# Loading 512 rows of w_down onto half of the partitions, in eight small transfers between the K and V loads

## The chip, the cores and the metric

One core of a Trainium2 chip runs the whole program. The metric is the device time of one execution in microseconds (us). On one core a run is called slow when it is over 1.5% above the fastest of its kernel, and such runs are left out of the ratios. The profile is one execution; its span is about 2 us shorter than the device time. All times on the traces' axis count from the start of the span. The traces name the engines PE (matmuls on TensorE), PEld (their weight loads), DVE (VectorE), ACT (ScalarE) and SP (which issues the loads). A "pair" is one weight load with the matmul that uses it.

## The reference

One decode step: 8 rows of x, attention with 32 query heads over the last 1024 positions of a K and V cache with 8 heads, and a gated feed-forward block whose result gates the attention.

```python
xn = layernorm(x)                                # [8, 1, 512]
q = xn @ wq                                      # 32 heads of 128
p = softmax(q @ k[last 1024].T / sqrt(128))      # 4 query heads share a K/V head
s = (p @ v) @ wo                                 # [8, 1, 512]
g = silu((gelu(xn @ w_gate) * (xn @ w_up)) @ w_down)   # F = 1792
out = x + s * g
```

Everything is bf16. There is little arithmetic and 47.5 MB to read: 16.8 MB each of K and V, 4.2 MB each of wq and wo, 1.8 MB each of w_gate, w_up and w_down.

## The kernel before

All loads are issued by one queue, in a fixed order: wq, then K and V in 1 MB pieces, then w_gate, w_up, the last V piece, w_down, and wo in four pieces. Eight semaphores take turns, so a load is issued when the one eight before it has landed.

```python
def load_rows(src, rows, r0, n, name):           # 128 partitions, n rows on each
    t = ring.tile([P, n, src.shape[1]], BF16, name=name, tag="slot")
    nc.sync.dma_start(out=t, in_=src.rearrange("(p r) n -> p r n", r=rows)[:, r0 : r0 + n, :])
    return t
...
wd_t = load_rows(B_w_down, FJ, 0, FJ, "wd_t")    # FJ = 14 rows on each partition
wo_t = [[load_rows(A_wo[: HT * Dh, :], WI, 0, WI, "wo_t")]]
wo_t.append([load_rows(A_wo[HT * Dh :, :], WI, 0, 8, "wo_t")])
...                                              # xr, then rows 8:13 and 13:16 of wo
```

Gate and up run as 14 groups of 128 columns of F. Since partition p of w_down's tile holds the rows 14p to 14p + 13, group j takes every 14th column:

```python
for w, wt in enumerate((wg_t, wu_t)):
    for j in range(FJ):
        for k in range(KD):                      # KD = 4
            nc.tensor.matmul(gu_ps[:, w, j, :],
                wt[:, k, :].rearrange("p (m j) -> p j m", j=FJ)[:, j, :],
                xnT[:, k, :], start=(k == 0), stop=(k == KD - 1))
```

GELU (ACT and DVE) makes hT of it, f_ps multiplies hT by w_down, and s_ps multiplies the attention output by wo, in the order in which wo's pieces land. Then two DVE instructions and the store end the program.

The softmax here doesn't subtract the row's maximum and nothing guards it: scores larger than these inputs give would overflow.

## Time and profile before

| | before |
|---|---|
| device time, median (range) | 122.9 us (122.73 to 123.09) |
| span of the profiled run | 121.0 us |
| DMA in the chain that ended last | 95% |
| PE busy | 85.1 us (70%) |
| last landing of the last wo piece | 116.86 us |
| gate starts / gate and up end | 96.26 / 104.06 us |
| s_ps ends | 117.44 us |

How to read it: 16 DMA engines work side by side (the page's DMA share is a mean over them). The records show sixteen increments of the semaphore for each load over 128 partitions, for the last wo piece from 113.73 to 116.86 us. They are read here as one from each engine, when its share of the load has landed: from 115 to 116 us, when nine of the sixteen have come (the ninth at 115.23), the DMA share is 0.42 of 16 engines, 6.7, and seven are missing. So the increments of one load say how far each engine is behind the others. These increments are in the trace's semaphore records; the page shows their sum only, as the way in which the DMA row falls at the end. The lines are in the prediction. No record numbers the engines. Where the texts give numbers, engines 0 to n - 1 are those that carry a load with n increments; that a load with more increments keeps the engines of one with fewer is the author's assumption.

### The profile page before, as it was taken

To read this page: it belongs to the slowest core of one execution; us is meant where nothing else is said; L and a number is where in the kernel's file an instruction comes from. 1 tells how busy PE (TensorE), PEld (TensorE's weight loads), DVE (VectorE), ACT (ScalarE), POOL (GpSimd) and SP (SyncE) were. 2 spreads that over 40 slices of the span, in tenths; PEclk is the share of its full clock that TensorE was granted. 3 is DMA by queue.
4 is the path that set the end of the run, shared out by engine and by line. 5 is a ranking of instruction groups with operands and counts; after the bars stand their busy time and mean duration, and the time that the engine had idled before them with its cause. 6 is when DMAs were issued, how large, how long until landed. Compare 5 with 4: busy or idle time off the path is not lost.

```text
span 121.0 us, 4362 instructions
## 1 busy us (share of the span) xinstructions
PE 85.1 (70%) x2015; PEld 78.7 (65%) x2030; DVE 69.8 (58%) x145; ACT 13.3 (11%) x22; POOL 1.4 (1%) x6
## 2 busy tenths in 40 slices
PE   0000699897879978879669693997969697845760
PEld 0000699896878977769669683896968597744640
DVE  3710036886947969669687592787859400398010
ACT  4500000110101101101101010110101100100000
POOL 4000000000000000000000000000000000000000
PEclk9999999999976999999999999599999955555555
DMA  4999999999999999999999999999999999999720
GB/s 100 423 433 433 401 420 420 433 423 431 417 428 423 420 431 415 428 423 428 423 420 417 431 425 428 428 423 420 417 449 433 418 419 440 438 417 409 316 88 3
DMA packets 6009, 47.75 MB, mean 395 GB/s; under 512 B 736, under 2 KB 744, under 8 KB 1000
## 3 DMA queue, kind: packets, MB, share of 16 engines
q1 hardware_dynamic: 5976, 47.47, 93.6%
q8 instruction: 16, 0.26, 0.8%
q10 hardware_dynamic: 16, 0.01, 0.0%
q14 instruction: 1, 0.01, 0.0%
HBM read 47.46 MB, written 0.01 MB: 392 GB/s over the span
## 4 chain that ended last, share of the span: by engine, by line
DMA 95%; DVE 0%; PE 0%; SPq 0%; issue 0%
DMA k_t<-in_A_k_cache_dram 51%; DMA wg_t<-in_B_w_gate_dram 18%; DMA wo_t<-in_A_wo_dram 17%; DMA wq_t<-in_A_wq_dram 10%; PE s_ps L355 0%; SPq L89 0%; DVE tmp L363 0%; DVE out_sb L365 0%; SPq L97 0%
## 5 line engine op out<-in xcount | busy, mean ns | idle before, releaser
L200 DVE COPY kT<-kT_ps 128x1024 bf16<-128x1024 bf16 x64 | 43.0, 692 | 16.0 <-PE kT_ps L196 16.0
L196 PE MATMUL kT_ps<-ident,k_t 128*128 128x128 bf16 x512 | 41.9, 230 | 11.8 <-DMA k_t<-in_A_k_cache_dram 11.8
L196 PEld LDWEIGHTS <-k_t 128*128 128x128 bf16 x512 | 31.8, 103 | 12.9 <-DMA k_t<-in_A_k_cache_dram 12.9
L213 PE MATMUL sc_ps<-qT,kT 128*128 128x16 bf16 x512 | 22.4, 170 | 0.5 <-DVE kT L200 0.4
L213 PEld LDWEIGHTS <-kT 128*128 128x128 bf16 x512 | 20.6, 98 | 2.9 <-issue 0.8
L220 ACT ACTIVATE pT<-sc_ps 128x512 bf16<-128x512 f32 x16 | 9.6, 597 | 80.8 <-PE sc_ps L213 80.8
L231 PEld LDWEIGHTS <-v_t 128*128 128x128 bf16 x512 | 15.5, 97 | 2.4 <-issue 0.8
L231 PE MATMUL oT_ps<-pT,v_t 128*128 128x16 bf16 x512 | 15.5, 170 | 1.3 <-issue 0.5
L235 DVE TENSOR_REDUCE sums<-sum_ps 128x16 f32<-128x512 f32 x16 | 11.0, 690 | 1.4 <-PE kT_ps L196 0.7
L178 PE MATMUL qT_ps<-xnT,wq_t 128*128 128x8 bf16 x128 | 3.7, 168 | 8.4 <-DMA wq_t<-in_A_wq_dram 8.4
L178 PEld LDWEIGHTS <-wq_t 128*128 128x128 bf16 x128 | 3.6, 104 | 8.5 <-DMA wq_t<-in_A_wq_dram 8.5
L207 PE MATMUL sc_ps<-mask,ident 128*128 128x512 bf16 x15 | 6.5, 430 | 0.0
L185 DVE CAST qT<-qT_ps 128x256 bf16<-128x256 f32 x1 | 0.4, 425 | 10.2 <-PE qT_ps L178 10.2
L355 PE MATMUL s_ps<-wo_t,oR 128*32 128x128 bf16 x128 | 4.2, 309 | 2.3 <-DMA wo_t<-in_A_wo_dram 2.3
L355 PEld LDWEIGHTS <-oR 128*32 128x32 bf16 x128 | 3.4, 139 | 2.9 <-issue 2.9
L290 DVE TENSOR_SCALAR z<-z 128x112 f32<-128x112 f32 x1 | 0.2, 219 | 8.4 <-ACT z L289 8.4
L239 DVE TENSOR_TENSOR oT<-oT_ps,sums 128x16 bf16<-128x16 f32 x16 | 3.7, 229 | 2.1 <-PE kT_ps L196 0.5
L238 DVE RECIPROCAL sums<-sums 128x16 f32<-128x16 f32 x16 | 4.0, 253 | 0.5
L279 PE MATMUL gu_ps<-xnT,wg_t 128*128 128x8 bf16 x56 | 3.5, 201 | 0.8 <-DMA wg_t<-in_B_w_gate_dram 0.8
L279 PE MATMUL gu_ps<-xnT,wu_t 128*128 128x8 bf16 x56 | 3.5, 202 | 0.7 <-DMA wu_t<-in_B_w_up_dram 0.7
L279 PEld LDWEIGHTS <-wg_t 128*128 128x128 bf16 x56 | 3.4, 161 | 0.9 <-DMA wg_t<-in_B_w_gate_dram 0.9
L279 PEld LDWEIGHTS <-wu_t 128*128 128x128 bf16 x56 | 3.5, 161 | 0.8 <-DMA wu_t<-in_B_w_up_dram 0.8
(51 smaller groups left out, 26.5 us busy)
## 6 DMA issues: line engine op xcount, KB each, us to landing
k_t<-in_A_k_cache_dram SPq DMA_DIRECT2D x16, 1024.0 KB, 20.5
v_t<-in_A_v_cache_dram SPq DMA_DIRECT2D x16, 1024.0 KB, 19.8
wq_t<-in_A_wq_dram SPq DMA_DIRECT2D x2, 2048.0 KB, 9.6
wo_t<-in_A_wo_dram SPq DMA_DIRECT2D x1, 2048.0 KB, 27.6
wg_t<-in_B_w_gate_dram SPq DMA_DIRECT2D x1, 1792.0 KB, 21.6
wu_t<-in_B_w_up_dram SPq DMA_DIRECT2D x1, 1792.0 KB
wd_t<-in_B_w_down_dram SPq DMA_DIRECT2D x1, 1792.0 KB, 25.2
wo_t<-in_A_wo_dram SPq DMA_DIRECT2D x1, 1024.0 KB, 27.4
```

Of the source, the lines that this page charges most:

```text
L178: nc.tensor.matmul(qT_ps[:, h, :], wq_t[k // 2][:, k % 2, h * Dh : (h + 1) * Dh], xnT[:, k, :], start=(k == 0), stop=(k == KD - 1),)
L196: nc.tensor.transpose(kT_ps[:, i * P : (i + 1) * P], k_t[b][:, h, t * TG + i, :], ident)
L200: nc.vector.tensor_copy(out=kT, in_=kT_ps)
L207: nc.tensor.matmul(sc[u].rearrange("p c h -> p (c h)"), ident, mask.rearrange("p c n j -> p (c n j)"), start=True, stop=False, skip_group_ ...
L213: nc.tensor.matmul(sc[u][:, t * TG + i, :], kTs[u, t][:, i * P : (i + 1) * P], qT[:, b, h * HS : (h + 1) * HS], start=False, stop=(t == NT ...
L220: nc.scalar.activation(out=pT[u], in_=sc[u], func=ACT.Exp, scale=inv_sqrt_dh)
L231: nc.tensor.matmul(oT_ps, v_t[b][:, h, c, :], pT[u][:, c, :], start=(c == 0), stop=(c == NCH - 1))
L235: nc.vector.tensor_reduce(out=sums, in_=sum_ps.rearrange("p c h -> p h c"), axis=AX.X, op=ALU.add)
L238: nc.vector.reciprocal(out=sums, in_=sums)
L239: nc.vector.tensor_tensor(out=oT[:, h, :, b], in0=oT_ps, in1=sums, op=ALU.mult)
L279: nc.tensor.matmul(gu_ps[:, w, j, :], wt[:, k, :].rearrange("p (m j) -> p j m", j=FJ)[:, j, :], xnT[:, k, :], start=(k == 0), stop=(k == K ...
L355: nc.tensor.matmul(s_ps[32 * q : 32 * (q + 1), :], oR[:, t, i, :], w[:, r, q * NW : (q + 1) * NW], start=(t == 0 and i == 0), stop=(t == N ...
```

## The change

The intent is to even out the ends of the DMA engines. Before, about half of them were done 3 us before the others (seven increments by 114.13 us, seven from 116.54 us on). 512 of w_down's rows now go by transfers of 8 partitions, which are carried by 8 engines only, and the 128-partition load of w_down shrinks by as much. The transfers are placed in the second half of the K and V loads, so that no engine runs far ahead. The partitions of each lie 4 apart.

```diff
-    FJ = F // P
+    FH = 64
+    FB = 8
+    FA = (F - FH * FB) // P
+    FJ = FA + FB
+    F0 = P * FA
...
+    wx_t = extra.tile([FH, FB, D], BF16, name="wx_t")
+    wx_rows = B_w_down[F0:, :].rearrange("(p j) n -> p (j n)", j=FB)
+    def load_extra(n):
+        p0 = 32 * (n // 4) + n % 4
+        nc.sync.dma_start(
+            out=wx_t[p0 : p0 + 29 : 4, :, :].rearrange("p j n -> p (j n)"),
+            in_=wx_rows[p0 : p0 + 29 : 4, :],
+        )
...
             load_cache(A_k_cache, u, k_t, "k_t")
+            if u >= NU - 8:
+                load_extra(u - (NU - 8))
             load_cache(A_v_cache, u - 1, v_t, "v_t")
...
-    wd_t = load_rows(B_w_down, FJ, 0, FJ, "wd_t")
+    wd_t = load_rows(B_w_down[:F0, :], FA, 0, FA, "wd_t")
...
+    nc.vector.memset(gu_ps[FH:P, :, FA:, :], 0.0)
...
+                if j < FA:
+                    cols = wt[:, k, :F0].rearrange("p (m j) -> p j m", j=FA)[:, j, :]
+                else:
+                    cols = wt[:, k, F0:].rearrange("p (m j) -> p j m", j=FB)[:, j - FA, :]
                 nc.tensor.matmul(
-                    gu_ps[:, w, j, :],
-                    wt[:, k, :].rearrange("p (m j) -> p j m", j=FJ)[:, j, :],
+                    gu_ps[: P if j < FA else FH, w, j, :],
+                    cols,
...
-                f_ps[...], hT[:, j, :], wd_t[:, j, q * NW : (q + 1) * NW],
+                f_ps[...],
+                hT[:, j, :] if j < FA else hT[:FH, j, :],
+                wd_t[:, j, ...] if j < FA else wx_t[:, j - FA, ...],
```

(One more line makes pT_pool 3 buffers instead of 4, for the room of wx_t.) Since the 512 rows lie on 64 partitions, 8 on each, the matmuls that make hT for them need weight loads of 64 columns, every eighth column of F.

More of the change, by code (lines that the diff above doesn't have):

```diff
@@ L63 @@
     ring = ctx.enter_context(tc.tile_pool(name="ring", bufs=10))
+    extra = ctx.enter_context(tc.tile_pool(name="extra", bufs=1))
     consts = ctx.enter_context(tc.tile_pool(name="consts", bufs=1))
     kT_pool = ctx.enter_context(tc.tile_pool(name="kT_pool", bufs=6))
-    pT_pool = ctx.enter_context(tc.tile_pool(name="pT_pool", bufs=4))
+    pT_pool = ctx.enter_context(tc.tile_pool(name="pT_pool", bufs=3))
     small = ctx.enter_context(tc.tile_pool(name="small", bufs=2))
@@ L326 @@
             nc.tensor.matmul(
-                f_ps[32 * q : 32 * (q + 1), :], hT[:, j, :], wd_t[:, j, q * NW : (q + 1) * NW],
+                f_ps[32 * q : 32 * (q + 1), :],
+                hT[:, j, :] if j < FA else hT[:FH, j, :],
+                wd_t[:, j, q * NW : (q + 1) * NW] if j < FA
+                else wx_t[:, j - FA, q * NW : (q + 1) * NW],
                 start=(j == 0), stop=(j == FJ - 1), tile_position=(0, 32 * q),
```

## The prediction

> **What bounds the kernel now.** I read the page's busy shares and slices first, then the chain of waits, the queues, the stretches of the last microseconds, the groups by shape, and the records of DMA packets and semaphore increments in the trace itself.
>
> The slices, the queues and the chain:
>
> ```profile
> PEclk9999999999976999999999999599999955555555
> DMA  4999999999999999999999999999999999999720
> ...
> q1 hardware_dynamic: 5976, 47.47, 93.6%
> q8 instruction: 16, 0.26, 0.8%
> q10 hardware_dynamic: 16, 0.01, 0.0%
> ...
> DMA 95%; DVE 0%; PE 0%; SPq 0%; issue 0%
> ```
>
> The 16 DMA engines are full from 3 us to about 113 us, and the chain is DMA for 95% of the span. PE is busy 70% and waits for data. So the kernel moves 47.5 MB at about 425 GB/s, and only bytes, or their division over engines, can move the end. The interesting part is the end of the DMA row: 9, 7, 2, 0. It doesn't drop at once. In stretches of 1 us (PE, PEld, DVE, ACT, POOL, clock, DMA share, GB/s):
>
> ```profile
> 113.00:114.00 1.00, 0.92 (x36) 0.73 (x28) 0.00 (x0) 0.00 (x0) 0.00 (x0) 0.50 0.77 302
> 114.00:115.00 1.00, 0.48 (x20) 0.48 (x23) 0.00 (x0) 0.00 (x0) 0.00 (x0) 0.50 0.54 223
> 115.00:116.00 1.00, 0.59 (x27) 0.40 (x20) 0.00 (x0) 0.00 (x0) 0.00 (x0) 0.50 0.42 170
> 116.00:117.00 1.00, 0.79 (x28) 0.59 (x31) 0.00 (x0) 0.00 (x0) 0.00 (x0) 0.50 0.15 58
> ```
>
> Half the engines are done by about 114 us, the other half at about 116.8 us (0.54 and 0.42 of 16 are 9 and 7 engines), although each was given the same bytes. The semaphore increments say it engine by engine. The last load (w_o, 384 KB) posts sixteen: seven at 113.73 to 114.13, one at 114.79, one at 115.23, seven at 116.54 to 116.86 us. For the K load at 15 us the sixteen lie within 0.4 us. The late ones split off one at a time in the first half, by 1.3 us each, and again in the second half, up to 3.1 us.
>
> The cause is in q8: 16 packets of 16 KB, about 6 us apart (18.6, 25.3, 31.3 ... 112.5, 117.0 us). Between two of them PE runs about 128 pairs of weight load and matmul, 256 instructions: they are PE's instruction fetches. Each takes about 0.93 us and slows the data packet beside it, and the engine that serves it falls 1.3 us behind. Fifteen fall before the data ends: seven engines get two, one gets one. That is exactly the late eight (seven at +2.8 us and the one at 115.23). The eighth early engine lost 0.7 us to one 8 KB fetch on another queue at 46.5 us.
>
> PE starts the last w_o rows when the slowest engine has landed them:
>
> ```profile
> 96.28 20.58 DMA wo_t<-in_A_wo_dram
> 116.86 0.04 issue
> 116.90 0.54 PE s_ps L355 x12
> 117.44 0.02 issue
> 117.46 0.30 DVE tmp L363
> ```
>
> 116.86 us is the end of the slowest engine; a fixed tail follows.
>
> [...]
> [...]x_sb (8 rows) is all of q10, 16 packets, 8 of data and 8 of semaphores. xr (source of outer size 4) posts four increments, at 111.43, 111.48, 111.69 and 112.39 us, with the early engines[...], the 0.7 us one among them. I choose to read the early eight as engines 0 to 7.
> [...]
> [...]
>
> **The change part by part.** *Bytes.* The total is the same. w_down on 128 partitions shrinks from 14 to 10 rows a partition: 4 KB less on each of 8 partitions of each engine, 32 KB less for all 16. The 512 rows on 64 partitions are 8 transfers of 8 packets of 8 KB: 64 KB more for each of engines 0 to 7. In the trace an 8 KB packet follows the one before on its engine by 0.306 us, with sometimes some 6 ns for the semaphore's. So:
> - late engines (8 to 15): 4 x 0.306 = 1.22 us less: 116.86 becomes 115.64.
> - early engines: 8 x 0.312 - 1.22 = 1.27 us more: the seven, 114.13 at most, become 115.4; the one that also served the 8 KB fetch, 114.79, becomes 116.06.
>
> In the tail a lone group of engines keeps the rate (170 GB/s at 0.42 x 16 engines is 25 GB/s each), so these shifts add. The end of data is the larger, 116.06, 0.80 us before now. The late group alone would have given 1.22 us; the one delayed early engine takes back 0.4.
>
> *Does the extra delay K and V?* Each load counts as landed with its slowest engine. From the ninth K on, extras add 0.31 us per 4.9 us; the late group's lead in lateness is 1.8 us at 54 us and 3.1 us at 69 us, and extras reach 2.5 us at about 90 us. For the 0.7 us engine that is 3.2 against 3.2. So no K or V lands later. The extra transfers also take three of every eight semaphore lanes, so the queue runs about 5.3 MB (13 us) ahead and not 8 MB (20 us); still ample.
>
> *PE.* Gate and up: 14 groups of j become 18 (10 of 128 columns, 8 of 64), each over 4 k, so 72 pairs per weight in place of 56: 40 full ones and 32 of 64 columns.
>
> ```profile
> L279 PE MATMUL gu_ps<-xnT,wg_t 128*128 128x8 bf16 x56 | 3.5, 201 | 0.8 <-DMA wg_t<-in_B_w_gate_dram 0.8
> L355 PE MATMUL s_ps<-wo_t,oR 128*32 128x128 bf16 x128 | 4.2, 309 | 2.3 <-DMA wo_t<-in_A_wo_dram 2.3
> L314 DVE TENSOR_TENSOR e<-o_sb,ownm 128x2048 bf16<-128x2048 bf16 x2 | 2.5, 1225 | 0.1
> ```
>
> A pair takes 3.52/56 = 63 ns. For a 64-column pair I take 57 ns as an estimate: 32 columns[...] take about 30 (s_ps, 1.90 us for 64 pairs), so 64 about double. 40 x 63 + 32 x 57 = 4.34 us in place of 3.52 per weight. The first 0.7 us of it falls into the wait for w_up, so gate and up end at 96.3 + 2 x 4.34 = 105.0, not 104.06. The memset of gu_ps (about 0.2 us on DVE, right after the last sums at 96.0) holds PE by 0.1 us at most. The GELU runs on 144 columns for 112: 32 more at about 1 ns in seven instructions, 0.2 us. f_ps gets 16 more pairs of 30 ns, 0.5 us, beside DVE's two e products. The matmuls of w_o could begin at 110.9 before (they waited until 112.03 for data); now at 110.9 + 0.95 + 0.25 = 112.1 to 112.3. Then 64 pairs to 114.2, 32 to 115.2, 20 to 115.9 (their data are there at 113.5 and 115.1), and the last 12 wait for 116.06. The new work costs slack, not time, but only some 0.2 us of slack is left.
>
> *Sum.* -0.80 us on the last landing, 0 to +0.2 for PE's shortened slack, the tail unchanged: 123.06 - 0.75 = 122.3 us.
>
> **The rivals.** (a) [...]512 KB on 8 engines takes 2.5 us there where 16 take 1.22: +1.2 us, about 124.3. It would hold if all engines ended together; the tail of shares above speaks against it.
> (b) *PE becomes the bound.* If a 64-column pair costs much more than 63 ns, say 80, gate and up end 1.5 us later again and the last w_o pairs are done at 118: 123.5 to 124. Against it: shorter loads elsewhere are never slower than 63 ns.
> (c) *The early group is not 0 to 7, or the fetches move.* Then the late engines get the extra: 116.86 + 1.27, 124.3. Against it: the four increments of xr. The 96 added PE instructions bring the sixteenth fetch forward to about 115 us, but it falls to the engine that has had one only, which is done at about 114.0; at worst 115.3, still under 116.06.
> (d) *Perfect balance.* If the 8 KB fetch falls on a late engine or is hidden, the end is 115.64, then PE binds at about 116.2 all the same: 122.1.
>
> **Range and chances.** The mechanism gives 122.1 to 122.5; the runs of before spread over 0.36 us, and PE's slack is thin on one side. So 122.3, with 121.9 to 122.8 for 8 in 10. Over 2% faster would be below 120.6, more than all the imbalance there is (the sixteen last increments average 115.3, 1.6 us before the latest): 1%. Over 2% slower, above 125.5, is beyond (a) to (c) singly: 2%. Within 2%: 97%.
>
> **What would show it.** Right: 8 wx_t transfers of 64 KB; the sixteen increments of the last load within about 1 us, the largest at about 116.0 and now from an early engine; DMA share near 0.9 until 115 us, then falling fast; K landings and the time of gate's start (96.3) unchanged; the last 12 pairs of s_ps starting at about 116.1 with a short wait for data. Wrong: an increment at 118 us or more (a, c); s_ps running without waits and ending after 117 (b); K landings later from 55 us on (extras not absorbed); gate starting clearly after 96.4 us (memset).

## The result

| | before | changed |
|---|---|---|
| device time, median (range) | 122.9 us (122.73 to 123.09) | 126.84 us (126.15 to 128.47, one of four slow) |
| span of the profiled run | 121.0 us | 124.4 us |
| last landing of the last wo piece | 116.86 us | 118.00 us |
| gate starts / gate and up end | 96.26 / 104.06 us | 97.01 / 109.76 us |
| s_ps ends | 117.44 us | 120.56 us |

The ratio is 1.030 (95% interval 1.023 to 1.038): slower. A ratio here is the mean time of one kernel's fast runs over that of the other's in the same rounds, so it isn't quite the ratio of the medians quoted.

The changed kernel's slices, and the first lines of the chain that ended last (shares by engine, then by line):

```profile
PE   0000899697697787976968759687597799975970
...
PEclk9999999999999999999999999999999755555555
DMA  4999999999999999999999999999999999998100
...
DMA 73%; PE 16%; SPq 4%; DVE 3%; issue 1%; ACT 1%; DVEq 0%
DMA k_t<-in_A_k_cache_dram 59%; DMA wg_t<-in_B_w_gate_dram 13%; PE gu_ps L303 10%; SPq L102 3%; PE s_ps L382 3%; PE f_ps L350 2%; SPq L94 1%; PE kT_ps L201 1%; PE r_ps L363 0%; DVE hT L325 0%; DVE sums L240 0%; DVE oR L367 0%; ACT th L320 0%; DVE u L324 0%; DVE u L318 0%
```

The DMA row still drops late, at 9, 8, 1, but the chain isn't DMA to the end any more. PE has come in with 16%. The chain in order of time (start, duration, what) shows where it changes over:

```profile
80.21 16.76 DMA wg_t<-in_B_w_gate_dram
96.96 0.05 issue
97.01 12.75 PE gu_ps L303 x144
...
111.75 0.47 DVE hT L325
...
113.65 2.16 PE f_ps L350 x52
115.80 0.54 PE r_ps L363 x16
...
116.93 3.63 PE s_ps L382 x128
...
120.59 0.30 DVE tmp L390
```

From 96.96 us, when w_gate lands, nothing waits for data. Gate and up take 12.75 us at one go, and all 128 pairs of s_ps run through in 3.63 us without a stop (before, they stopped four times for wo's pieces). The groups by shape say which of gate's and up's instructions do it (operation, tiles, shapes, count, then busy us and mean ns of one, then idle time before):

```profile
L303 PE MATMUL gu_ps<-xnT,wg_t 128*64 128x8 bf16 x32 | 4.0, 262 | 0.0
L303 PE MATMUL gu_ps<-xnT,wu_t 128*64 128x8 bf16 x32 | 4.0, 262 | 0.0
L303 PEld LDWEIGHTS <-wg_t 128*64 128x64 bf16 x32 | 3.9, 216 | 0.0
...
L382 PE MATMUL s_ps<-wo_t,oR 128*32 128x128 bf16 x128 | 3.6, 312 | 0.1
L303 PE MATMUL gu_ps<-xnT,wg_t 128*128 128x8 bf16 x40 | 2.5, 199 | 1.1 <-DMA wg_t<-in_B_w_gate_dram 1.1
...
L363 PE MATMUL r_ps<-selb,e 128*128 128x8 bf16 x32 | 1.1, 169 | 0.0
```

Busy time divided by count is the spacing of pipelined pairs (the mean of one, 262 ns for a narrow pair, is longer, since they overlap). The 40 full pairs take 2.5 us, 62 ns a pair, as before (63). The 32 narrow ones, with half the columns, take 4.0 us: 125 ns a pair, twice as long as the full ones. (The last line is for later: r_ps's 128 weight columns are neighbours, and its pairs take 34 ns.) The idle time of s_ps, 0.1 us, is what is left of 2.3 us before.

The loads didn't become better either. The sixteen increments of the last wo piece, and the eight of the first extra transfer, from the semaphore records:

```
last wo piece, before   113.73 113.76 113.85 113.89 113.91 114.05 114.13 114.79 115.23 116.54 116.57 116.66 116.67 116.76 116.79 116.86
last wo piece, changed  112.68 112.85 114.15 114.22 115.06 115.23 115.29 115.30 115.35 115.41 115.43 115.56 115.59 116.01 117.95 118.00
first extra transfer    52.25 52.31 52.41 52.50 52.51 53.19 53.80 53.85
```

Fourteen of the sixteen now end by 116.01 us, as intended. Two end at 118.0, later than any before, and two at 112.7 and 112.9, without any delay at all. The first extra transfer explains it: of its eight engines five are on time, one is 0.7 us late (it served an 8 KB fetch at 46.4 us), and two are 1.3 us late. Two engines that serve PE's instruction fetches are among the eight that carry the extra rows, and two that don't are left out.

### The profile page after: what moved, and what is told of

It is laid out like the page before. It is cut to its first block, busy times and chain, and to the rows that moved or that the text cites.

```text
span 124.4 us, 4469 instructions
## 1 busy us (share of the span) xinstructions
PE 88.3 (71%) x2063; PEld 82.5 (66%) x2078; DVE 69.9 (56%) x146; ACT 13.3 (11%) x22; POOL 1.4 (1%) x6
## 4 chain that ended last, share of the span: by engine, by line
DMA 73%; PE 16%; SPq 4%; DVE 3%; issue 1%; ACT 1%; DVEq 0%
DMA k_t<-in_A_k_cache_dram 59%; DMA wg_t<-in_B_w_gate_dram 13%; PE gu_ps L303 10%; SPq L102 3%; PE s_ps L382 3%; PE f_ps L350 2%; SPq L94 1%; PE kT_ps L201 1%; PE r_ps L363 0%; DVE hT L325 0%; DVE sums L240 0%; DVE oR L367 0%; ACT th L320 0%; DVE u L324 0%; DVE u L318 0%
## 5 line engine op out<-in xcount | busy, mean ns | idle before, releaser
L201 PE MATMUL kT_ps<-ident,k_t 128*128 128x128 bf16 x512 | 39.9, 223 | 15.0 <-DMA k_t<-in_A_k_cache_dram 15.0
L201 PEld LDWEIGHTS <-k_t 128*128 128x128 bf16 x512 | 30.1, 99 | 16.3 <-DMA k_t<-in_A_k_cache_dram 16.3
L218 PEld LDWEIGHTS <-kT 128*128 128x128 bf16 x512 | 20.1, 96 | 2.5 <-DVE kT L205 0.5
L303 PE MATMUL gu_ps<-xnT,wg_t 128*128 128x8 bf16 (+1 forms) x72 | 6.4, 227 | 1.1 <-DMA wg_t<-in_B_w_gate_dram 1.1
L303 PEld LDWEIGHTS <-wg_t 128*128 128x128 bf16 (+1 forms) x72 | 6.3, 183 | 1.2 <-DMA wg_t<-in_B_w_gate_dram 1.2
L303 PE MATMUL gu_ps<-xnT,wu_t 128*128 128x8 bf16 (+1 forms) x72 | 6.4, 227 | 0.0
L303 PEld LDWEIGHTS <-wu_t 128*128 128x128 bf16 (+1 forms) x72 | 6.3, 183 | 0.0
L212 PE MATMUL sc_ps<-mask,ident 128*128 128x512 bf16 x15 | 5.9, 395 | 0.0
L382 PE MATMUL s_ps<-wo_t,oR 128*32 128x128 bf16 x128 | 3.6, 312 | 0.1
```

Source lines behind the costliest of these rows:

```text
L201: nc.tensor.transpose(kT_ps[:, i * P : (i + 1) * P], k_t[b][:, h, t * TG + i, :], ident)
L212: nc.tensor.matmul(sc[u].rearrange("p c h -> p (c h)"), ident, mask.rearrange("p c n j -> p (c n j)"), start=True, stop=False, skip_group_ ...
L218: nc.tensor.matmul(sc[u][:, t * TG + i, :], kTs[u, t][:, i * P : (i + 1) * P], qT[:, b, h * HS : (h + 1) * HS], start=False, stop=(t == NT ...
L303: nc.tensor.matmul(gu_ps[: P if j < FA else FH, w, j, :], cols, xnT[:, k, :], start=(k == 0), stop=(k == KD - 1),)
L382: nc.tensor.matmul(s_ps[32 * q : 32 * (q + 1), :], oR[:, t, i, :], w[:, r, q * NW : (q + 1) * NW], start=(t == 0 and i == 0), stop=(t == N ...
```

## The experiments

Two theories stood against each other after the result: (A) the narrow weight loads made PE the bound, and the loads' two late engines cost something besides; (B) the loads are the whole loss, or none of it. All kernels below differ from one of the two by what is shown. The ratios are read by their 95% intervals, none of which includes 1.

### The loads of the change with the PE work of before

```diff
-    FJ = FA + FB
+    FJ = F // P                                  # gate, up and f_ps as before
...
+                hT[:, j, :],
+                wd_t[:, j % FA, q * NW : (q + 1) * NW],
```

The result is wrong: the extra rows are loaded and not used. ("Result right" below rests on reading the code.)

> Loads as in the changed kernel, PE work as before (14 groups of 128 columns, no memset; result wrong on purpose, since f_ps reads w_down rows twice and not the extra ones). Theory (the new 64-column pairs made PE the bound, and apart from that the new loads end late on two engines): the last load still lands at about 118.0 us as in the changed kernel, the last 12 pairs wait for it, span about 119.2 + 3 = 122.2, time about 124.1, 1% slower than before. Rival (the loads are all right, as the prediction had it, and only PE is slow): last landing about 116.1, time 122.1, faster than before. Rival (the loads are the whole loss): time 126 or more.

Measured: 124.08 us (123.96 to 124.29), ratio 1.010 (1.008 to 1.012). The chain's end:

```profile
80.29 18.00 DMA wg_t<-in_B_w_gate_dram
...
98.34 19.45 DMA wo_t<-in_A_wo_dram
117.80 0.04 issue
117.84 0.54 PE s_ps L376 x12
```

The last landing is 117.80 us (two increments at 117.71 and 117.80, the others at most 115.92). So the loads alone lose 1%. The prediction that the loads gain is refuted, and so is the rival that they are the whole loss. In this fast run w_gate landed as late as 98.28 us, since both of the two engines had served their second fetch by then (the V piece before it has their increments at 93.99 and 94.04 us; in the changed kernel's profile both came by 92.71).

### The PE work of the change with balanced loads: two attempts

First attempt: the 512 rows by one transfer over 64 partitions, beside w_down's load.

```diff
-    def load_extra(n): ...
     wd_t = load_rows(B_w_down[:F0, :], FA, 0, FA, "wd_t")
+    nc.sync.dma_start(out=wx_t.rearrange("p j n -> p (j n)"), in_=wx_rows)
```

> PE work as in the changed kernel, but the 512 rows are loaded by one transfer over 64 partitions beside the w_down load[...]. Theory: last landing as before, about 116.9; gate and up 6.3 us each from 96.3 us, ending at 109.0; s_ps then ends about 119.9; span 123.6, time about 125.6, PE-bound. Rival (the loads are the whole loss): time as before, 123.

Measured: 127.44 us (127.27 to 127.94), ratio 1.038. It didn't isolate what it was to isolate, for the loads themselves became slower. The stretches (us, then PE, PEld, DVE, ACT, POOL busy, clock, DMA share, GB/s):

```profile
100.00:102.00 2.00, 2.00 (x19) 2.00 (x19) 0.00 (x0) 0.00 (x0) 0.00 (x0) 0.50 1.03 437
102.00:104.00 2.00, 2.00 (x32) 1.98 (x31) 0.00 (x0) 0.00 (x0) 0.00 (x0) 0.50 1.11 309
105.00:106.00 1.00, 1.00 (x10) 1.00 (x10) 0.00 (x0) 0.00 (x0) 0.00 (x0) 0.50 1.09 219
109.00:110.00 1.00, 1.00 (x30) 0.80 (x29) 0.54 (x2) 0.29 (x2) 0.00 (x0) 0.50 1.00 229
```

The DMA engines stay busy (a share of 1.00 to 1.12), but from 102 to 110 us they move about half: 309 GB/s at first, then 207 to 246. An 8 KB packet takes 0.45 to 1.0 us there and 0.309 elsewhere. By these rates 2.0 MB moved in the 8 us, where 425 GB/s would have moved 3.4 MB. The transfer is at most 0.5 MB of it, so the loads next to it suffered too, and the last landing came at 121.2 us, 4.4 us later than before. What slows the engines beside such a transfer is not shown. The eight transfers of the change, with 8 partitions each, 4 apart, show no such loss: the changed kernel moves 422 to 426 GB/s in each 10 us from 50 to 90 us.

Second attempt: all loads exactly as before, the narrow f_ps matmuls read rows of w_down's tile (wrong result).

```diff
-    def load_extra(n): ...
-    wd_t = load_rows(B_w_down[:F0, :], FA, 0, FA, "wd_t")
+    wd_t = load_rows(B_w_down, F // P, 0, F // P, "wd_t")
...
+                else wd_t[:FH, FA + (j - FA) % 4, q * NW : (q + 1) * NW],
```

> PE and DVE work as in the changed kernel, all loads exactly as before (w_down on 128 partitions; the narrow f_ps matmuls read rows of it, so the result is wrong on purpose). This is what the run with one 64-partition transfer was to show and didn't, since that transfer itself slowed the loads. Theory: last landing about 116.9 us as before, gate and up 6.35 us each from 96.3, s_ps done about 119.8, PE-bound, span 123.6, time about 125.5. Rival (the PE work costs nothing by itself): 123.

Measured: 125.13 us (124.80 to 125.37), ratio 1.016 (1.013 to 1.019). The groups and the end of the chain:

```profile
L290 PE MATMUL gu_ps<-xnT,wg_t 128*64 128x8 bf16 x32 | 4.0, 261 | 0.0
...
L290 PE MATMUL gu_ps<-xnT,wg_t 128*128 128x8 bf16 x40 | 2.4, 198 | 0.8 <-DVE gu_ps L282 0.8
```

```profile
116.08 3.63 PE s_ps L369 x69
119.74 0.30 DVE tmp L377
```

PE is the bound with the loads of before. For the two profiled executions (125.36 and 126.15 us) the sum now closes. Gate starts at 96.20 us in this run and at 97.01 in the changed kernel (0.81 us later), and tmp starts at 119.74 and 120.59 (0.85 later). So of the 3.1 us that s_ps ends later than before, 2.3 are the PE work by itself (119.7 for 117.44) and 0.8 the later start of gate, which comes from the loads: PE-bound, the kernel passes on every delay of w_gate. (The medians differ by more, 1.7 us, since the gate of the changed kernel starts later in some executions; see its second profile below.) The line also shows that the memset releases gate here ("<-DVE gu_ps"), within 0.1 us of when w_gate would have.

### Why a narrow pair takes 125 ns: width or stride

Two runs take one property away each. In the first the 64 columns are neighbours (wrong result):

```diff
-                    cols = wt[:, k, F0:].rearrange("p (m j) -> p j m", j=FB)[:, j - FA, :]
+                    cols = wt[:, k, F0 + (j - FA) * FH : F0 + (j - FA + 1) * FH]
```

> As the changed kernel, but the 64-column weight loads read 64 neighbouring columns instead of every eighth (result wrong on purpose). If both the narrow load and the stride make a pair slow: a pair falls from about 119 ns to about 57 (twice the 30 ns of the 32-column contiguous ones), gate and up 4.3 us each, PE no longer binds, time 124.1 with the end at the late loads (118.0). If the column count alone is the cause: a pair stays at about 119 ns and the time at 126.2.

In the second the extra block is the first 512 rows of w_down, so that the same every-eighth pattern can run over 128 columns, of which the first 64 are used and the rest computed and ignored. No memset is needed, and the result is right (by reading the code):

```diff
-    F0 = P * FA
+    F0 = FH * FB                                 # extra block first
-    nc.vector.memset(gu_ps[FH:P, :, FA:, :], 0.0)
...
+                    cols = wt[:, k, : P * FB].rearrange("p (m j) -> p j m", j=FB)[:, j - FA, :]
-                    gu_ps[: P if j < FA else FH, w, j, :],
+                    gu_ps[:, w, j, :],
```

> As the changed kernel, but the extra block is the first 512 rows and its weight loads take 128 columns, every eighth, of which only 64 are used; no memset; result right. If the narrow width is what makes a pair slow: pairs of 63 ns as the others, gate and up 4.5 us each, end at the late loads, time about 124.1. If the stride of eight is the cause: pairs of 120 ns or more, time 126 or more.

Measured: 124.27 us (124.02 to 125.13), ratio 1.013, and 124.03 us (123.95 to 124.12), ratio 1.009. The groups of the first run, then of the second:

```profile
L303 PE MATMUL gu_ps<-xnT,wg_t 128*128 128x8 bf16 x40 | 2.5, 199 | 0.9 <-DMA wg_t<-in_B_w_gate_dram 0.9
...
L303 PE MATMUL gu_ps<-xnT,wg_t 128*64 128x8 bf16 x32 | 1.9, 195 | 0.0
```

```profile
L302 PE MATMUL gu_ps<-xnT,wg_t 128*128 128x8 bf16 x72 | 4.4, 200 | 1.1 <-DMA wg_t<-in_B_w_gate_dram 1.1
```

A pair takes 59 ns with 64 neighbouring columns, 61 ns with 128 columns of every eighth and tenth, and 125 ns with 64 columns of every eighth. Beside the 34 ns of r_ps (128 neighbouring columns) these four show that each property alone nearly doubles a pair, and both together nearly quadruple it. The kernel before had the stride already; the change added the narrow width on top. With either of them taken away the kernel is back at the end that its loads set: 124.0 to 124.3 us, as with the PE work of before. So the narrow strided loads were the whole of the PE part, and repairing them leaves the 1% that the loads lose. The runs show the times, not the mechanism.

### Which engines serve the fetches

Six small loads of 5, 6, 7, 10, 12 and 14 rows are put between the last K and V loads of the kernel before, results unused.

```diff
+    PROBES = [5, 6, 7, 10, 12, 14]
+    def probe(n):
+        t = probe_pool.tile([PROBES[n], D], BF16, name="probe_t")
+        nc.sync.dma_start(out=t, in_=B_w_down[: PROBES[n], :])
...
+            if u >= NU - 6:
+                probe(u - (NU - 6))
```

> The kernel before with six small loads of 5, 6, 7, 10, 12 and 14 rows between the last K and V loads, results unused. Each should post as many semaphore increments as it has rows[...], each increment as late as its engine is behind. An engine that serves PE's instruction fetches is 1.3 us late or more. In the changed kernel two of the eight engines of an extra transfer were late[...] the 5-, 6- and 7-row loads say which: if they are 6 and 7, the 5- and 6-row loads post no late increment and the 7-row load one. Time as before, 123 to 123.5.

The increments of the first three, from the semaphore records (the others are summed up below):

```
5 rows   61.79 61.95 62.00 62.03 62.72
6 rows   66.74 66.90 67.00 67.04 67.68 68.32
7 rows   71.78 71.90 71.97 72.08 72.64 73.28 73.35
```

Each load posts one increment a row (5, 6 and 7 here), which is read as n engines for n rows. With 5 rows nobody is late but the 8 KB one (0.7 us); the sixth row brings one that is 1.3 us late, the seventh another. The eight rows of the change add one that is on time. If each of these loads keeps the engines of the smaller ones, as the numbering assumes, engines 5 and 6 serve fetches, not 6 and 7, the case that the expectation had spelled out. So engines 0 to 7 are six early ones and two late ones. The three larger loads say more: of the 10-row load 3 increments are late by about 1.3 us or more, of the 12-row load 5, of the 14-row load 7. By the same reading the late engines are 5, 6, one of 8 and 9, 10 to 13, and one of 14 and 15: eight in all.

The time of this one run, 125.3 us (123 to 123.5 expected), isn't used: from 88 us on all packets took about 10% longer than before (0.59 us for 14 KB in place of 0.54), also where no probe was near. Why, stays open.

### Fewer extra rows: eight engines against five

256 rows (4 on each of 64 partitions), with the full-width repair. Once by the change's eight transfers of 8 partitions, once by transfers of 5 partitions, which engines 0 to 4 carry (5 rows posted five increments in the probe run):

```diff
-    FB = 8
+    FB = 4                                       # both
...
-        p0 = 32 * (n // 4) + n % 4               # with five engines only:
+        rows = slice(n, n + 49, 12) if n < 12 else slice(60, 64)
...
-            if u >= NU - 8:
-                load_extra(u - (NU - 8))
+            if u >= NU - 13:
+                load_extra(u - (NU - 13))
```

> The same 256 extra rows and the same PE work, but by eight transfers of 8 partitions 4 apart, so by engines 0 to 7. Engines 5 and 6 serve fetches and get 8 x 0.16 - 0.61 = 0.67 us more: last landing 117.5, time 123.6, ratio about 1.005, with two late increments at 117.5 and none other above 116.3. If engines 5 and 6 don't matter: as with five engines or better, 122.4.

> As the run with the extra block first and full 128-column weight loads, but 256 extra rows (64 partitions of 4 rows), loaded by twelve transfers of 5 partitions 12 apart and one of 4, so by engines 0 to 4 alone; result right. If engines 5 and 6 of the eight spoiled the change's loads: the late group loses 16 KB an engine, 0.61 us, and lands at 116.25; the early engine that served the 8 KB fetch gains 12 x 0.16 - 0.61 = 1.3 us and something for the last transfer, about 116.3; gate and up 64 pairs of 62 ns, PE not bound; time 122.4 to 122.6, ratio about 0.996. If the lag of the engines has another cause than the instruction fetches of fixed engines, or extras cost more than their packets: 123 or more.

Measured with eight: 123.52 us (123.32 to 123.78), ratio 1.005 (1.003 to 1.006). The end of its chain:

```profile
117.34 0.04 issue
117.38 0.53 PE s_ps L381 x11
```

117.34 us for 117.5 expected, by two increments (117.23 and 117.34); the other fourteen are at most 116.14. The arithmetic of packets per engine holds. One thing in this run did not come as assumed (62 ns for every pair): its 48 pairs with every twelfth column start 59 to 61 ns apart, but its 16 pairs with every fourth column 33 ns, as if the columns were neighbours.

Measured with five: 123.76 us (123.33 to 124.91), ratio 1.008. This expectation failed. All engines were late, the clean ones too. The stretches show when:

```profile
50.00:60.00 10.00, 7.17 (x182) 6.65 (x181) 7.35 (x14) 1.19 (x2) 0.00 (x0) 1.00 1.02 397
60.00:70.00 10.00, 8.65 (x194) 7.98 (x194) 7.65 (x14) 1.19 (x2) 0.00 (x0) 0.83 1.01 382
70.00:80.00 10.00, 8.66 (x185) 8.09 (x188) 6.74 (x13) 1.19 (x2) 0.00 (x0) 0.83 1.01 420
```

For some 20 us the engines were full and moved 7 to 10% less than the 427 GB/s of the kernel before from 60 to 70 us (0.345 us for an 8 KB packet in place of 0.31), as in the probe run. The runs with transfers on 8 engines don't show it. Both that do have transfers on 5 and other numbers of engines, but what causes it was not found. The spread of the five-engine runs (1.6 us) is large, and the profiled one (124.63 us) is among the slower; even the fastest (123.33) missed the expected 122.4 to 122.6. One of the five engines also lost 1.3 us at 46 us, where 0.7 was expected.

### Moving bytes at the end of the kernel before

The last test keeps the kernel before and cuts only the last wo piece (3 rows on each partition), so that most of it is carried by five engines (85 rows; that they are five is the author's assumption) or by seven (119 rows; seven increments, below), 17 packets each:

```diff
-    wo_t[1].append(load_rows(A_wo[HT * Dh :, :], WI, 13, 3, "wo_t"))
+    wo_last = ring.tile([P, 3, D], BF16, name="wo_t", tag="slot")
+    for p0, p1 in ((0, 32), (32, 43), (43, 128)):     # or ((0, 9), (9, 128))
+        nc.sync.dma_start(out=wo_last[p0:p1], in_=wo_rows[p0:p1, 13:16, :])
+    wo_t[1].append(wo_last)
```

> The kernel before, with only the last w_o load (3 rows of 128 partitions) cut: 32 partitions on 16 engines, 11 on engines 0 to 10, 85 on engines 0 to 4 (17 packets of 3 KB each); result right. Theory (fetches make fixed engines late, 0 to 4 are not among them): the late group loses 8 packets of 0.121 us and gets 3, last landing 116.86 - 0.60 = 116.25; the engine with the 8 KB fetch gets 3 + 17 - 8 = 12 packets more, 114.79 + 1.45 = 116.25; time 122.4, ratio 0.995. [...]

> The same cut with 9 partitions on engines 0 to 8 and 119 on engines 0 to 6, again 17 packets an engine. Engines 5 and 6 are among the late ones: 116.86 + (1 + 17 - 8) x 0.121 = 118.1, time 124.2, ratio 1.010. If it only matters how many bytes an engine gets: not slower than with five engines, 122.4.

Measured: 124.11 us (123.86 to 124.64), ratio 1.011, and 125.10 us (124.93 to 125.62), ratio 1.018. With seven, the increments of the large part are 115.78, 115.82, 115.98, 116.58, 117.43, 119.01 and 119.12: the two late engines stand out by 1.6 us and more, and the second kernel is 1 us slower than the first for them. That part holds. Both are 0.8 to 1.6% slower than expected, though: with five, the last increment came at 117.66 us for 116.25. The stretches with five:

```profile
113.00:114.00 1.00, 0.95 (x36) 0.75 (x29) 0.00 (x0) 0.00 (x0) 0.00 (x0) 0.50 0.86 230
114.00:115.00 1.00, 0.00 (x0) 0.00 (x0) 0.00 (x0) 0.00 (x0) 0.00 (x0) 0.50 0.77 189
115.00:116.00 1.00, 0.44 (x20) 0.44 (x23) 0.00 (x0) 0.00 (x0) 0.00 (x0) 0.50 0.69 172
```

From 114 to 115 us a DMA share of 0.77 moves 189 GB/s, where before 0.54 moved 223: busy engines that move little, as with the 64-partition load. The cause was not tested by itself. No version beat the kernel before.

### The change once more

> The changed kernel itself once more, for its spread (126.15 to 128.47 so far) and a second profile. Theory: s_ps runs without a wait for data, gate begins at about 97.0, 6.35 us for each weight, last landing 118.0, time 126.2 where TensorE's granted clock falls to half at about 96 us and not earlier; the slower ones have their half-clock stretches elsewhere.

Measured: 127.64 us (126.14 to 129.37, three of six slow), ratio of the fast runs 1.028 (1.026 to 1.031). The profiled run is a slow one and is not used to explain the loss. As expected, each weight took 6.35 us (12.70 for both), s_ps ran without a wait for data, and the last landing was at 117.98 us. But gate began at 99.56 us and not at about 97.0. The last K piece landed at 91.45 us (89.94 in the first profile), then the granted clock was at half from 92 to 94 us, and the memset behind the sums of this late group released gate at 99.5 us, 1.1 us after w_gate had landed (98.44).

The late landings aren't bound to the slow state, since the fast run with the loads alone has them too (w_gate at 98.28 us). What differs is the place of the two engines in the round of fetches. In these two runs one of the two engines falls behind a second time after the fetch at 84.5 us (85.0 in the slow run), the other after the one at 90.6 us (90.7), so both before w_gate lands. In the changed kernel's first profile this happens after the fetches at 97.1 and 106.4 us, both after w_gate has landed. This fits the large spread of a PE-bound kernel next to the 0.3 us of the loads alone; why the round starts at another engine is open.

## Why the prediction was wrong

**The step that failed** is the PE part: "For a 64-column pair I take 57 ns as an estimate". The estimate doubled the 30 ns of s_ps's pairs of 32 columns (1.90 us for 64 of them). So it came from contiguous weight loads and was applied to strided ones. Contiguous, it is right: 59 ns measured. Strided by eight, a pair takes 125 ns. Gate and up took 12.75 us in place of the predicted 2 x 4.34 = 8.68, so 4.1 us more, and started 0.7 us later: they ended at 109.76 us, not at 105.0. The slack of "some 0.2 us" that the prediction had counted left no room for it.

**The rival that came true** is (b), with a larger price than it named: 80 ns was its case, 125 the fact. The argument used against it, "shorter loads elsewhere are never slower than 63 ns", rests on loads like those of s_ps, whose weights are contiguous. The full strided pair (63 ns) against the contiguous one of v_t (1.04 us for 32 pairs, 32 ns) already showed in the profile before that the stride costs a factor of two. Multiplying the two, 57 x 2, would have given 114 ns. The sum for 80 ns was itself too high: uninterrupted, the 128 pairs of s_ps take 3.63 us and not the 4.2 of four separate groups, so starting 1.5 us later than the predicted 112.2, at 113.7 us, they would have ended at 117.3, hardly later than before. The slack was larger than the prediction said, by some tenths of a microsecond, and 125 ns still broke it.

**The step on the engines** failed too: "I choose to read the early eight as engines 0 to 7." xr's four increments spoke for four engines only; the rest was chosen. Two of the eight, 5 and 6 by the reading of the probe, are late ones. They got 1.27 us more on top of two fetches, and ended at 118.0 in place of 116.06. From this follows that "no K or V lands later" is wrong as well: the last V before w_gate landed at 92.71 us (91.86 before), w_gate at 96.96 (96.22). Alone this would have cost 1.0%, so the sign of the prediction was wrong in the loads too. It was (c) of the rivals, for two engines of eight; the increments told of it, the DMA row didn't.

**What held.** The instruction fetches put engines behind by about 1.3 us each (shown by the times of fetches and late increments; no run changed the number of fetches). In the kernel before, the fifteen fetches of 16 KB before the data end take 0.88 to 0.97 us each, and beside each of the first eleven one 8 KB packet takes 0.77 to 0.86 us in place of 0.31. From one fetch to the next 202 to 301 recorded instructions of PE and PEld start, 249 in the mean. The bytes per engine add as computed (the engine with the 8 KB fetch was expected at 116.06 us and came at 116.01, the other late ones at 115.64 and came by 115.6); the total of bytes and the rate are unchanged; the memset costs 0.1 us at most in the fast profiles. The GELU on 144 columns took what was said (0.2 us more in its seven instructions; hT 0.47 us for 0.40).

**The range.** It took both DMA and PE terms as known to a few tenths, from one estimate each that nothing in the profile had measured. A chance of 2% for slower was far too small for a kernel in which the change added 64 pairs of a shape that did not yet occur, beside 0.2 us of slack.

## What to carry to other kernels

Before moving work to fewer partitions, look at what it does to the shape of the matmuls that use them: pairs whose weight load is both narrow and strided took twice the time of full strided ones here (125 ns for 61 to 63), and loading 128 columns and ignoring half of the result was faster (61 ns a pair). The stride itself is worth a look: every eighth column and more cost 58 to 63 ns a pair here, every fourth 33. When DMA engines end apart, find out by their semaphore increments which engines are behind before choosing which get more; small loads of n rows can tell (of the probes here, 5 rows had no increment that was 1.3 us late, 6 rows one, 7 rows two). A kernel bound by loads has slack on its other engines only up to a number that can be read off the idle time before the last group (2.3 us here), so compare every added instruction with it.
